# Attention with a gated MLP, one core: the steps of the plans in another order

## The chip, the cores and the metric

The kernel runs on one core of a Trainium2 chip. The metric is the device time of one execution in microseconds. The kernel before was timed in 11 runs; their median is 251.98 us, and they lie between 251.03 and 254.94 us. A separate execution was profiled: it gave the trace and the page of figures that this document reads.

The core has one engine for matrix products (PE, TensorE), with a part that loads its weights (PEld), two engines for elementwise work (DVE, VectorE, and ACT, ScalarE), a general one (POOL, GpSimd) and one that here only issues transfers (SP, SyncE). Each engine takes its instructions in a fixed order from its own queue. Engines wait for each other through semaphores.

## The reference

The inputs are q (8 batches, 16 heads, 384 positions, 64 wide), k and v (4 heads of the same size, each shared by four q heads), and the weights of a gated MLP: w_in 1024x1024, w_spatial 384x384 with a bias of 384, w_out 512x1024. Everything is float32. Cut to what matters:

```python
attn  = softmax(q @ k.T / 8)              # each k, v head serves four q heads
x     = (attn @ v), heads side by side    # [8, 384, 1024]
h     = relu(x @ w_in)                    # [8, 384, 1024]
u, v  = h[..., :512], h[..., 512:]
v_n   = (v - mean(v)) / sqrt(var(v) + 1e-6)      # over the 512
v_s   = w_spatial @ v_n + b_spatial       # mixes the 384 positions
out   = (u * v_s) @ w_out                 # [8, 384, 1024]
```

## The kernel before

**Plans.** The order of the work is written out by hand, as three strings of steps. `FIRST` holds batches 0 to 2 with the loading of the weights; `STEADY` is one repeating batch, run with the base batch 3, 4, 5 and 6; `LAST` is batch 7 and what is left of batch 6. `run` (lines 728 to 736) takes the steps of a string one after the other and calls a function for each. In a step such as `oc,-2,3,v` the first number is the batch relative to the base, and a letter at the end is the engine: v for DVE, s for ACT, p for POOL. All of it stands under a manual schedule, so each engine's queue holds its instructions exactly in the order of the plan. No scheduler moves anything. A step that stands earlier in the string stands earlier in its own engine's queue, and only there.

**What the steps do.** For each batch:
- `lq`, `lk`, `lv` load q (two halves of 8 heads), k and v in float32; they are issued on SP's queue. Each has one staging buffer, so a load waits until the casts of the batch before have read that buffer. `cq`, `ck`, `cv` cast to float16. `dk`, `dq` transpose k and q by DMA from SP's queue. The first two batches transpose on PE instead (`Tq`, `Tk`, with `tq`, `tk` to copy the result out of PSUM).
- `S` computes scores (two matmuls of 512 columns, line 367), `E` takes their exponentials on ACT (line 380). There are 18 of each per batch. They go through two score buffers in PSUM, so a score waits for the exponential two before it.
- `X` (lines 384 to 395) multiplies the exponentials with v for a tile of 128 positions. Parts 0 and 1 are the two halves of v's columns; part 2 multiplies with ones and so makes the sums of the softmax. All of them use strips of 32 columns of the array, so that four heads run side by side (line 394). `rl` and `re` make the reciprocal of the sums on ACT as exp(-ln) (lines 405 and 411), `rv` makes one on DVE, and `xm` multiplies a part with it on DVE (line 423).
- V is the half of h that becomes v; `ru` its relu (DVE line 448 or ACT line 450), `bs` its statistics (458, 459), `rs` the reciprocal root, `nm` the normalisation (469). `sa` adds the bias to the spatial product on DVE (495), `gt` is relu of u times v_s on DVE (521), `oc` copies a piece of the output out of PSUM (325 on ACT, 327 on DVE), `st` stores a pair of pieces from SP (563), and `lo` is the last piece.
- `lwi`, `lws`, `lwo` load the weights; `cws`, `cwo` cast them. w_out has two staging buffers for its four parts.

**Paired matmuls.** In a `G` step (lines 677 to 688) two streams of matmuls that use 64 rows each run at the same time in the upper and the lower half of the array. A `G` has two phases with two parts each. `w12`, `w24` and `w10` pair V of one tile (line 599) with two pieces of output of an earlier batch (line 639): `w12` is tile 2 of the batch before with pieces 2 and 3 of the batch before that, and so on. `gs` pairs spatial products (625), `gu` U products (612), `go` output products. The second phase swaps the halves of the array and must not begin before the first has ended. A mark (`mk`) sees to that:

```python
693: done = nc.vector.memset(mark_v[:, 0:1], 0.0)
695: done = nc.gpsimd.memset(mark_p[:, 0:1], 0.0)
```

The mark waits for the last matmul of the first phase, and the first matmul of the second phase waits for the mark. It stands in the queue of DVE or POOL like any other instruction: what is ahead of it delays it, and what is behind it waits for it.

**PSUM banks.** The results of `X`, V, U, spatial and output products share four banks. `bank` (lines 168 to 172) hands out the bank that was freed first, in the order in which the steps that read the results stand in the plan (`read`, lines 174 to 177). So which bank a product gets, and what it waits for, is settled by the order in the plan. Three buffers hold pairs of output pieces on their way to the store.

Of the kernel before, what the change touches and what calls it, by code (L numbers as in the profile page):

```python
# [774 lines left out]
```

## Time and profile before

| | us |
|---|---|
| median of 11 runs | 251.98 |
| lowest, highest | 251.03, 254.94 |
| the profiled execution, whole | 251.01 |
| its span in the trace | 249.2 |
| X,0,0,2 of batches 3, 4, 5, 6 starts at | 86.75, 115.20, 143.73, 172.33 |
| X,0,0,2 of the last batch starts at | 200.93 |
| last matmul ends | 244.98 |
| last store has landed | 248.07 |

The span runs from the first instruction to the last in the trace. The profiled execution took 1.81 us more than its span, which is what lies before and behind. A line of the profile's groups gives the line of the kernel, the engine, the operation, its output and inputs with their sizes, how often it ran, how long it was busy in all and on average, and how long the engine had been idle before it and for whom. A line of the timeline gives the start, the length and the same names, and, in brackets, the idle time just before. "Busy" of PE counts overlapping matmuls once. A row of the table by stretch gives the stretch, its length, the busy time and number of instructions of PE, PEld, DVE, ACT and POOL, then the granted clock of TensorE, the share of the 16 DMA engines' time and GB/s. "DMA" and "PEclk" in the page are tenths over 40 equal slices.

### The profile page before, as it was taken

The numbers are of one execution on the slowest core, as the hardware profiler recorded it, in microseconds if no ns is written. First come the engines' busy times: TensorE is split into PE (matmuls) and PEld (weight loads), VectorE is DVE, ScalarE is ACT, GpSimd is POOL, SyncE is SP. The second block draws the span as 40 slices with busy tenths as digits, with TensorE's granted clock in tenths as the row PEclk, the third lists the DMA queues.
The fourth block names the chain that finished last, engine by engine and source line by source line (L and its number), as shares of the span: only waits on it lengthen the run. The fifth ranks groups of instructions, "written<-read, shape, count | busy, mean of one in ns | idle before, by whom it ended". The sixth has DMA issues, their size and how long they took to land.

```text
span 249.2 us, 5953 instructions
## 1 busy us (share of the span) xinstructions
PE 238.4 (96%) x2505; PEld 122.2 (49%) x2505; DVE 148.4 (60%) x291; ACT 183.4 (74%) x231; POOL 48.2 (19%) x94
## 2 busy tenths in 40 slices
...
PEclk9999999999999999999999999999999999999999
DMA  7999999998799384771939366690932022200606
GB/s 184 272 253 321 188 255 292 235 312 143 88 323 325 93 206 122 239 227 73 208 116 308 93 163 166 178 284 13 200 120 87 3 84 87 85 3 0 252 0 252
DMA packets 57610, 42.71 MB, mean 171 GB/s; under 512 B 26864, under 2 KB 53872, under 8 KB 57584
## 3 DMA queue, kind: packets, MB, share of 16 engines
...
q14 instruction: 7, 0.06, 0.1%
...
## 4 chain that ended last, share of the span: by engine, by line
PE 91%; ACT 3%; DVE 2%; DMA 1%; issue 1%; ACTq 0%
PE X L394 20%; PE po L639 14%; PE sc L367 14%; PE pu L612 13%; PE pv L599 11%; PE pv L437 5%; PE psp L625 4%; PE po L544 4%; PE pu L509 4%; ACT aT L380 3%; DMA q<-in_q_dram 1%; DVE v_s L495 1%; PE pq L348 1%; PE psp L483 1%; PE sc_u L509 1%
## 5 line engine op out<-in xcount | busy, mean ns | idle before, releaser
L380 ACT ACTIVATE aT<-sc 128x1024 f16<-128x1024 f32 x144 | 140.2, 1025 | 28.0 <-PE sc L367 27.8
L639 PE MATMUL po<-w_out,gT 64*128 64x512 f16 x288 | 68.2, 376 | 0.0
L599 PE MATMUL pv<-w_in,xt 64*128 64x512 f16 x272 | 64.9, 376 | 0.0
L367 PE MATMUL sc<-qT,kT 64*128 64x512 f16 x288 | 54.8, 390 | 1.1 <-ACT aT L380 0.6
L327 DVE COPY osb<-po 128x512 f32<-128x512 f32 x39 | 26.9, 688 | 20.1 <-PE po L639 17.5
L394 PE MATMUL X<-aT,v 128*32 128x512 f16 x576 | 36.1, 380 | 0.0
L423 DVE TENSOR_TENSOR xt<-X,rec 128x512 f16<-128x512 f32 x48 | 31.1, 685 | 7.5 <-ACT rec L411 4.3
L612 PE MATMUL pu<-xt,w_in 64*128 64x384 f16 x384 | 35.4, 322 | 0.0
L639 PEld LDWEIGHTS <-gT 64*128 64x128 f16 x288 | 25.3, 94 | 14.6 <-DVE mark_v L693 3.0
L599 PEld LDWEIGHTS <-xt 64*128 64x128 f16 x272 | 24.7, 94 | 12.7 <-issue 4.2
L521 DVE SCALAR_TENSOR_TENSOR gT<-pu,v_s 128x384 f16<-128x384 f32 x31 | 16.1, 554 | 24.9 <-PE pu L612 21.1
L327 POOL CAST q<-q 128x768 f16<-128x768 f32 (+2 forms) x32 | 23.5, 761 | 32.1 <-DMA q<-in_q_dram 32.0
L367 PEld LDWEIGHTS <-kT 64*128 64x128 f16 x288 | 16.9, 94 | 24.2 <-issue 13.9
L612 PEld LDWEIGHTS <-w_in 64*128 64x128 f16 x384 | 18.8, 94 | 13.5
L495 DVE TENSOR_TENSOR v_s<-psp,bias_b 128x384 f32<-128x384 f32 x32 | 20.1, 689 | 6.1 <-PE psp L483 3.4
L394 PEld LDWEIGHTS <-v 128*32 128x32 f16 x576 | 15.9, 96 | 15.2 <-issue 2.6
L695 POOL MEMSET mark_p<- 1x1 f32 x18 | 1.6, 89 | 104.5 <-PE psp L625 64.5
L405 ACT ACTIVATE rec<-X 128x512 f32<-128x512 f32 x23 | 13.8, 599 | 9.2 <-PE X L394 8.5
L394 PE MATMUL X<-aT,ones 128*32 128x512 f16 x288 | 20.1, 382 | 0.5 <-DVE v_s L495 0.2
L458 DVE BATCH_NORM_STATS2 stats<-v_r 128x6 f32<-128x512 f32 x24 | 16.5, 689 | 5.5 <-ACT v_r L450 2.9
L625 PE MATMUL psp<-wsT,v_n 64*128 64x384 f16 x144 | 15.3, 323 | 0.1
L411 ACT ACTIVATE rec<-rec 128x512 f32<-128x512 f32 x23 | 14.5, 630 | 0.6
...
## 6 DMA issues: line engine op xcount, KB each, us to landing
...
```

Of the source, the lines that this page charges most:

```text
L327: engine.tensor_copy(dst, src)
L367: nc.tensor.matmul(sc[:, half, 0 : 512 // js], kT[b][lo:hi, gp, t, :], qT[b, gp][lo:hi, qt, j0::js], start=True, stop=True,)
L380: nc.scalar.activation(aT[b, qt][:, gp, t].rearrange("p h (j q) -> p h j q", j=G)[:, :, j0::js], held["sc", b, u, j0][:, :, 0 : 512 // js] ...
L394: nc.tensor.matmul(dst[32 * g : 32 * (g + 1), :], v16[:, g, t, 32 * part : 32 * (part + 1)] if part < 2 else ones32, a[:, g // 2, t, g % 2 ...
L423: nc.vector.tensor_tensor(xt[:, jj, :, qt * P : (qt + 1) * P], held["X", b, qt, jj].rearrange("p (j q) -> p j q", j=G), held["rec", b, qt] ...
L458: nc.vector.bn_stats(s6, held["v_r", b, st])
L495: nc.vector.tensor_tensor(held["v_s", b][:, m, :].rearrange("p (t s) -> p t s", t=NST), held["psp", b, m][:, 0:S].rearrange("p (t s) -> p ...
L521: nc.vector.scalar_tensor_tensor(held["gT", b][:, mu, :], held["pu", b, mu][:, 0:S], 0.0, held["v_s", b][:, mu, :], op0=ALU.max, op1=ALU.mult,
L599: yield lambda kc=kc: nc.tensor.matmul(held["pv", b, st], xT[b][rows, kc, st * P : (st + 1) * P], w_in16[rows, kc, DH:DFF], start=(first a ...
L612: yield lambda kc=kc: nc.tensor.matmul(held["pu", b, mu][:, 0:S], w_in16[rows, kc, mu * P : (mu + 1) * P], xT[b][rows, kc, :], start=(firs ...
L625: yield lambda st=st: nc.tensor.matmul(held["psp", b, m][:, 0:S], held["v_n", b, st][rows, m * P : (m + 1) * P], wsT16[rows, st, :], start ...
L639: yield lambda m=m: nc.tensor.matmul(held["po", b, i], held["gT", b][rows, m, tt * P : (tt + 1) * P], w_out16[rows, m, half * 512 : (half ...
```

## The change

Only the three strings differ. The set of steps is the same in each string, apart from the engine of some of them; what differs is their order.

In `STEADY`: `X,0,0,0` still follows the sums, but `X,0,0,1` is moved behind the first w phases, into the next tile; the parts of the next tile run as sums, the rest of the tile before, then its own; the scores `S` are spread in another way. The q casts are four as before, but one is on DVE instead of POOL and stands ahead of the w12 mark; one `ck` is on ACT instead of POOL; `ru,-1,2` and `oc,-2,3` are on ACT instead of DVE; the mark of `gs,2` is on DVE instead of POOL. `cv,1` is moved from the head of the batch to behind the mark of `gu,2` on POOL. The loads `lq,2,0`, `lv,2`, `lk,2` and `lq,2,1` are moved from the middle of the batch to its end, with v ahead of k, and the stores `st,-2` behind them.

In `LAST`: the products V of tiles 1 and 2 stand ahead of U of the batch before. U, spatial and output products of batches 6 and 7 stand in another order, and the stores are collected near the end; `st,0,1` comes after `lo`.

In `FIRST`: the first k and q loads change places, and so do the halves of the first casts; `lv,1` is ahead of q of batch 1; k of batch 2 is behind its q; w_out's loads come later, and so do their eight casts, six of them on POOL and two on DVE instead of six on POOL and two on ACT; the order of scores, exponentials and X parts differs throughout.

```diff
--- before
+++ after
 FIRST = """
-lq,0,0,0,1,0,1,s lk,0,0,2 cq,0,0,0,1,0,0,1,v lq,0,1,0,1 lk,0,2,4 ck,0,0,0,3,p cq,0,0,0,1,1,0,1,s
-Tq,0,0,0,0,1 Tk,0,0,0,3 tq,0,0,0,0,1,s lq,0,0,1,3 lq,0,1,1,3 tk,0,0,0,3,v S,0 ck,0,1,0,3,v
-cq,0,1,0,1,1,0,1,v cq,0,1,0,1,0,0,1,p lv,0 lk,1 S,0 lwi,0,1,0 lwi,0,1,2 Tk,0,1,0,3 lq,1,0 lq,1,1
-lws,0 cq,0,0,1,3,1,0,1,p lbi,0 lk,2 lv,1 Tq,0,1,0,0,1 lq,2,0 lwi,0,1,3 lwi,0,1,1 cq,0,1,1,3,0,0,1,p
-cq,0,1,1,3,1,0,1,p cv,0,p tk,0,1,0,3,v S,0 tq,0,1,0,0,1,v lq,2,1 lwo,0,1 cq,0,0,1,3,0,0,1,v E,0 E,0
...
-S,0 Tq,0,1,1,0,1 S,0 Tq,0,1,2,0,1 E,0 S,0 tq,0,1,2,0,1,v tq,0,1,1,0,1,v X,0,0,2 lwo,0,0
...
-cq,2,0,0,3,0,0,1,p cq,2,1,0,3,1,0,1,p cwo,0,1,1,p cwo,0,1,0,p cq,2,1,0,3,0,0,1,p xm,0,1,0 S,0
-tk,1,0,0,3,v cq,1,0,0,1,1,0,1,v cwo,0,0,0,p cwo,0,0,1,p S,0 E,0 Tk,1,1,0,3 V,0,1,0,4 Tq,1,0,0,0,1
...
-tq,1,1,1,0,1,s X,1,0,0 S,0 dk,2 bs,0,2 tw,0,0,2 dq,2,0 bs,0,0 S,0 X,1,0,1 Tq,1,1,2,0,1 rl,1,0 re,1,0
-lwo,0,3 lwo,0,2 xm,1,0,0 E,0 rs,0 xm,1,0,1 S,0 E,0 V,1,0,0,4 E,0 nm,0,0 nm,0,2 tq,1,1,2,0,1,v
-V,1,0,4,8 S,0 S,0 nm,0,1 G,0,gs,2,0,0,1 E,0 dq,2,1 ru,1,0,v E,0 G,0,gs,0,0,0,1 mk,0,gs,2,v
-mk,0,gs,0,v G,0,gs,2,1,0,1 S,0 G,0,gs,0,1,0,1 S,0 sa,0,2 sa,0,3 sa,0,0 sa,0,1 lk,3 lv,2 E,0 X,1,1,2
...
-G,0,gu,0,1,0 S,0 E,0 E,0 S,0 G,0,gu,0,1,1 G,0,gu,2,1,1 gt,0,1 gt,0,2 gt,0,3 E,0 E,0 S,0 cwo,0,3,0,p
-cwo,0,2,0,p X,1,2,2 X,1,2,1 V,1,1,0,4 V,1,1,4,8 S,0 E,0 rl,1,2 cwo,0,3,1,s gt,0,0 cwo,0,2,1,s re,1,2
-E,0 G,0,go,0,0,0 G,0,go,0,0,1 S,0 E,0 E,0 ru,1,1,v mk,0,go,0,v G,0,go,0,1,0 S,0 ck,3,0,0,3,p
...
-oc,0,2,v xm,2,0,0 G,1,w12,2,1,1 S,0 dk,3 dq,3,0 dq,3,1 lk,4 X,2,1,2 oc,0,3,v ru,1,2,v bs,1,2 X,2,1,1
...
-S,0 oc,1,0,v xm,2,2,0 X,2,2,1 st,0,1 st,0,0 E,0 lv,3 lq,4,0 st,0,2 ru,2,1,v oc,1,1,v lq,4,1 lv,4
...
+lk,0,0,2 lq,0,0,0,1,0,1,s cq,0,0,0,1,1,0,1,s lq,0,1,0,1 cq,0,0,0,1,0,0,1,v lk,0,2,4 ck,0,0,0,3,p
+Tq,0,0,0,0,1 Tk,0,0,0,3 tq,0,0,0,0,1,s lq,0,0,1,3 lq,0,1,1,3 tk,0,0,0,3,v lk,1 lv,0 ck,0,1,0,3,p S,0
+S,0 lv,1 Tk,0,1,0,3 cq,0,1,0,1,0,0,1,p cq,0,1,0,1,1,0,1,p lq,1,0 lws,0 lq,1,1 Tq,0,1,0,0,1 lbi,0
+lq,2,0 lq,2,1 lk,2 lwi,0,1,0 lwi,0,1,1 tk,0,1,0,3,v cq,0,0,1,3,1,0,1,p lwi,0,1,3 lwi,0,1,2
+tq,0,1,0,0,1,v cq,0,0,1,3,0,0,1,v E,0 S,0 S,0 ck,1,0,0,3,p ck,1,1,0,3,p cv,0,p Tq,0,0,2,0,1 E,0 E,0
...
+Tq,1,1,2,0,1 re,1,0 xm,1,0,0 S,0 E,0 xm,1,0,1 rs,0 E,0 nm,0,0 lwo,0,1 dq,2,0 nm,0,1 tq,1,1,2,0,1,v
+nm,0,2 lwo,0,0 dk,2 dq,2,1 lwo,0,2 lwo,0,3 V,1,0,0,4 lv,2 V,1,0,4,8 E,0 S,0 G,0,gs,2,0,0,1 S,0
...
+E,0 sa,0,3 sa,0,1 X,1,1,2 sa,0,0 E,0 rl,1,1 X,1,1,1 X,1,1,0 S,0 lq,3,1 lk,3 lq,3,0 re,1,1 E,0
...
+cwo,0,0,0,v G,0,gu,2,1,0 cwo,0,1,0,p cwo,0,0,1,p mk,0,gu,0,p cwo,0,1,1,p S,0 G,0,gu,0,1,0 S,0
+G,0,gu,0,1,1 E,0 gt,0,1 S,0 cwo,0,2,0,p E,0 G,0,gu,2,1,1 gt,0,2 gt,0,3 bs,1,0 gt,0,0 cwo,0,3,0,v E,0
+cwo,0,2,1,p S,0 X,1,2,2 X,1,2,1 E,0 cwo,0,3,1,p S,0 S,0 V,1,1,0,4 E,0 V,1,1,4,8 E,0 rl,1,2 S,0
+G,0,go,0,0,0 G,0,go,0,0,1 S,0 E,0 E,0 re,1,2 xm,1,2,1 mk,0,go,0,v E,0 G,0,go,0,1,0 E,0 S,0
...
+rl,2,1 bs,1,2 xm,2,0,1 re,2,1 S,0 xm,2,1,1 G,2,w24,0,0,0 G,2,w24,0,0,1 rs,1 S,0 E,0 S,0 E,0 E,0 lv,3
+xm,2,1,0 mk,2,w24,0,v dk,3 dq,3,0 dq,3,1 nm,1,2 nm,1,0 nm,1,1 G,2,w24,0,1,0 oc,0,4,v G,2,w24,0,1,1
...
+G,2,w10,1,1,1 S,0 X,2,2,1 E,0 oc,1,1,s lk,4 st,0,0 lq,4,0 st,0,2 lq,4,1 ru,2,1,v xm,2,2,1 oc,1,0,v
+st,0,1 E,0 bs,2,1 st,1,0 lv,4
 """
...
 STEADY = """
-X,0,0,2 rl,0,0 re,0,0 X,0,0,0 X,0,0,1 S,0 E,0 xm,0,0,0 xm,0,0,1 ck,1,0,0,3,p ck,1,1,0,3,p
-cq,1,0,0,3,0,0,1,p cq,1,0,0,3,1,0,1,p cq,1,1,0,3,0,0,1,p cq,1,1,0,3,1,0,1,p cv,1,p dk,1 dq,1,0
-dq,1,1 G,-1,w12,2,0,0 G,-1,w12,2,0,1 mk,-1,w12,2,v S,0 E,0 S,0 E,0 G,-1,w12,2,1,0 oc,-2,2,v
-G,-1,w12,2,1,1 ru,-1,2,v oc,-2,3,v st,-2,1 bs,-1,2 X,0,1,2 rl,0,1 re,0,1 X,0,1,0 X,0,1,1 rs,-1 S,0
-E,0 xm,0,1,0 xm,0,1,1 nm,-1,0 nm,-1,1 G,0,w24,0,0,0 G,0,w24,0,0,1 mk,0,w24,0,v nm,-1,2 S,0 E,0 S,0
-E,0 G,0,w24,0,1,0 oc,-2,4,v G,0,w24,0,1,1 ru,0,0,s oc,-2,5,v st,-2,2 bs,0,0 lk,2 lq,2,0 lq,2,1 lv,2
-S,0 E,0 G,-1,gs,0,0,0,1 mk,-1,gs,0,p S,0 E,0 G,-1,gs,2,0,0,1 mk,-1,gs,2,p G,-1,gs,0,1,0,1 sa,-1,0
-sa,-1,1 S,0 E,0 G,-1,gs,2,1,0,1 sa,-1,2 sa,-1,3 X,0,2,2 rl,0,2 re,0,2 X,0,2,0 X,0,2,1 S,0 E,0
-xm,0,2,0 xm,0,2,1 G,-1,gu,0,0,0 G,-1,gu,0,0,1 mk,-1,gu,0,p S,0 E,0 G,-1,gu,2,0,0 G,-1,gu,2,0,1
-mk,-1,gu,2,p S,0 E,0 G,-1,gu,0,1,0 G,-1,gu,0,1,1 gt,-1,0 gt,-1,1 S,0 E,0 G,-1,gu,2,1,0 G,-1,gu,2,1,1
-gt,-1,2 gt,-1,3 S,0 E,0 S,0 E,0 G,0,w10,1,0,0 G,0,w10,1,0,1 mk,0,w10,1,v S,0 E,0 S,0 E,0
-G,0,w10,1,1,0 oc,-1,0,v G,0,w10,1,1,1 ru,0,1,v oc,-1,1,v st,-1,0 bs,0,1 S,0 E,0
+X,0,0,2 cq,1,0,0,3,1,0,1,p cq,1,1,0,3,0,0,1,p cq,1,1,0,3,1,0,1,v X,0,0,0 rl,0,0 S,0 G,-1,w12,2,0,0
+G,-1,w12,2,0,1 cq,1,0,0,3,0,0,1,p ck,1,1,0,3,p dq,1,1 re,0,0 E,0 ck,1,0,0,3,s S,0 mk,-1,w12,2,v dk,1
+dq,1,0 S,0 G,-1,w12,2,1,0 G,-1,w12,2,1,1 E,0 xm,0,0,0 oc,-2,2,v X,0,1,2 E,0 ru,-1,2,s rl,0,1
+oc,-2,3,s re,0,1 X,0,0,1 X,0,1,0 bs,-1,2 xm,0,0,1 X,0,1,1 S,0 xm,0,1,0 G,0,w24,0,0,0 G,0,w24,0,0,1
+rs,-1 nm,-1,1 xm,0,1,1 mk,0,w24,0,v nm,-1,0 nm,-1,2 S,0 E,0 S,0 G,0,w24,0,1,0 oc,-2,4,v
+G,0,w24,0,1,1 E,0 E,0 S,0 G,-1,gs,0,0,0,1 S,0 ru,0,0,s mk,-1,gs,0,p oc,-2,5,v E,0 G,-1,gs,2,0,0,1
+bs,0,0 mk,-1,gs,2,v G,-1,gs,0,1,0,1 E,0 sa,-1,1 G,-1,gs,2,1,0,1 S,0 sa,-1,2 sa,-1,3 sa,-1,0 X,0,2,2
+rl,0,2 X,0,2,0 X,0,2,1 S,0 G,-1,gu,0,0,0 G,-1,gu,0,0,1 S,0 re,0,2 E,0 E,0 xm,0,2,0 xm,0,2,1 E,0
+G,-1,gu,2,0,0 G,-1,gu,2,0,1 S,0 mk,-1,gu,0,p E,0 G,-1,gu,0,1,0 G,-1,gu,0,1,1 S,0 E,0 mk,-1,gu,2,p
+cv,1,p G,-1,gu,2,1,0 G,-1,gu,2,1,1 S,0 S,0 gt,-1,0 gt,-1,1 gt,-1,3 gt,-1,2 G,0,w10,1,0,0
+G,0,w10,1,0,1 E,0 S,0 E,0 mk,0,w10,1,v S,0 G,0,w10,1,1,0 G,0,w10,1,1,1 oc,-1,0,v oc,-1,1,v ru,0,1,v
+lq,2,0 lv,2 lk,2 S,0 lq,2,1 st,-2,2 st,-2,1 E,0 E,0 E,0 bs,0,1 st,-1,0
 """
 
 LAST = """
-X,0,0,2 rl,0,0 re,0,0 X,0,0,0 X,0,0,1 S,0 E,0 xm,0,0,0 xm,0,0,1 G,-1,w12,2,0,0 G,-1,w12,2,0,1
-mk,-1,w12,2,v S,0 E,0 S,0 E,0 G,-1,w12,2,1,0 oc,-2,2,v G,-1,w12,2,1,1 ru,-1,2,v oc,-2,3,v st,-2,1
-bs,-1,2 X,0,1,2 rl,0,1 re,0,1 X,0,1,0 X,0,1,1 rs,-1 S,0 E,0 xm,0,1,0 xm,0,1,1 nm,-1,0 nm,-1,1
-G,0,w24,0,0,0 G,0,w24,0,0,1 mk,0,w24,0,v nm,-1,2 S,0 E,0 S,0 E,0 G,0,w24,0,1,0 oc,-2,4,v
-G,0,w24,0,1,1 ru,0,0,s oc,-2,5,v st,-2,2 bs,0,0 S,0 E,0 V,0,1,0,4 V,0,1,4,8 ru,0,1,s bs,0,1 SP,-1,0
-sa,-1,0 SP,-1,1 sa,-1,1 SP,-1,2 sa,-1,2 SP,-1,3 sa,-1,3 X,0,2,2 rl,0,2 re,0,2 X,0,2,0 X,0,2,1
-xm,0,2,0 xm,0,2,1 U,-1,0 gt,-1,0 U,-1,1 gt,-1,1 U,-1,2 gt,-1,2 U,-1,3 gt,-1,3 V,0,2,0,4 V,0,2,4,8
-ru,0,2,s bs,0,2 rs,0 nm,0,0 nm,0,1 nm,0,2 O,-1,0 oc,-1,0,s O,-1,1 oc,-1,1,s st,-1,0 O,-1,2 oc,-1,2,s
-O,-1,3 oc,-1,3,s st,-1,1 O,-1,4 oc,-1,4,s O,-1,5 oc,-1,5,s st,-1,2 U,0,0,1 SP,0,0 sa,0,0 gt,0,0
-SP,0,1 sa,0,1 SP,0,2 sa,0,2 SP,0,3 sa,0,3 U,0,1 gt,0,1 U,0,2 gt,0,2 U,0,3 gt,0,3 O,0,0,0,3 O,0,1,0,3
-O,0,0,3,4 oc,0,0,v O,0,1,3,4 oc,0,1,s st,0,0 O,0,2 oc,0,2,v O,0,3 oc,0,3,s st,0,1 O,0,4 oc,0,4,v
-st,0,2,0,512 lo,0,5
+S,0 X,0,0,2 E,0 G,-1,w12,2,0,0 G,-1,w12,2,0,1 S,0 mk,-1,w12,2,v S,0 E,0 rl,0,0 re,0,0 G,-1,w12,2,1,0
+G,-1,w12,2,1,1 S,0 X,0,1,2 oc,-2,2,v X,0,0,1 oc,-2,3,v rl,0,1 re,0,1 E,0 ru,-1,2,v X,0,1,1 X,0,0,0
+xm,0,0,1 xm,0,1,1 X,0,1,0 xm,0,0,0 S,0 G,0,w24,0,0,0 G,0,w24,0,0,1 E,0 mk,0,w24,0,v E,0 S,0 S,0 E,0
+bs,-1,2 xm,0,1,0 G,0,w24,0,1,0 G,0,w24,0,1,1 E,0 oc,-2,4,v ru,0,0,s X,0,2,2 rl,0,2 re,0,2 rs,-1
+oc,-2,5,s X,0,2,0 X,0,2,1 xm,0,2,0 xm,0,2,1 nm,-1,0 V,0,1,0,4 V,0,1,4,8 V,0,2,0,4 nm,-1,1 nm,-1,2
+U,-1,1 V,0,2,4,8 ru,0,1,s SP,-1,0 SP,-1,1 bs,0,0 ru,0,2,v sa,-1,0 sa,-1,1 bs,0,2 gt,-1,1 bs,0,1
+U,-1,0 SP,-1,2 SP,-1,3 rs,0 nm,0,1 sa,-1,2 sa,-1,3 nm,0,0 nm,0,2 gt,-1,0 U,0,0,1 U,-1,2 gt,-1,2
+U,-1,3 SP,0,2 gt,-1,3 sa,0,2 SP,0,3 O,-1,4 U,0,2 SP,0,0 sa,0,3 sa,0,0 O,-1,2 O,-1,0 oc,-1,4,v gt,0,2
+O,-1,1 oc,-1,0,s oc,-1,1,s O,-1,5 O,-1,3 SP,0,1 oc,-1,5,v oc,-1,2,v sa,0,1 U,0,1 U,0,3 gt,0,0 gt,0,1
+gt,0,3 oc,-1,3,s st,-2,2 O,0,0,0,3 st,-2,1 st,-1,2 O,0,4 O,0,1,0,3 oc,0,4,s O,0,0,3,4 O,0,1,3,4
+st,-1,1 st,-1,0 oc,0,1,v oc,0,0,s O,0,2 O,0,3 oc,0,2,s oc,0,3,s st,0,2,0,512 st,0,0 lo,0,5 st,0,1
 """
```

## The prediction

> **What bounds the kernel now.** I read the page first, then the busy times by stretch, then TensorE's timeline of one repeating batch, and last the queues that feed it.
>
> ```profile
> span 249.2 us, 5953 instructions
> PE 238.4 (96%) x2505; PEld 122.2 (49%) x2505; DVE 148.4 (60%) x291; ACT 183.4 (74%) x231; POOL 48.2 (19%) x94
> ...
> PEclk9999999999999999999999999999999999999999
> DMA  7999999998799384771939366690932022200606
> ...
> PE 91%; ACT 3%; DVE 2%; DMA 1%; issue 1%; ACTq 0%
> ```
>
> TensorE holds 91% of the chain at full granted clock. The DMA row is at nines up to 60 us, and loose afterwards. The busy times by stretch:
>
> ```profile
> 115.20:143.80 28.60, 28.54 (x333) 15.69 (x336) 17.72 (x35) 22.26 (x27) 5.24 (x11) 1.00 0.66 174
> 143.80:172.40 28.60, 28.54 (x333) 15.69 (x336) 17.72 (x35) 22.26 (x27) 5.24 (x11) 1.00 0.62 173
> ```
>
> A repeating batch takes 28.60 us. Since matmuls overlap, "28.54 busy" hides waits, so I sum the issue spacings instead: a 512-column pair or round is 0.216, a 384-column pair 0.1625, a switch between X (32-column strips) and anything else about 0.1 (X from 143.73 to the score at 145.79: 2.06 for 9 rounds, 1.94). A batch is 9 X parts at 0.65, 18 scores at 0.216, six w phases at 1.73, four gs phases at 0.49, four gu phases at 1.30: 27.22, with six switches 27.8. So **0.8 us of each batch are waits**, and only these can be won. TensorE's timeline of the batch that starts at 143.73 shows where:
>
> ```profile
> 146.02 0.38 PE L639 MATMUL po<-w_out,gT 64*128 64x512 f16 x1
> 146.24 0.38 PE L639 MATMUL po<-w_out,gT 64*128 64x512 f16 x1
> ...
> 146.79 0.37 PE L639 MATMUL po<-w_out,gT 64*128 64x512 f16 x1
> ...
> 158.74 0.72 PE L625 MATMUL psp<-wsT,v_n 64*128 64x384 f16 x6
> 159.52 0.83 PE L394 MATMUL X<-aT,ones 128*32 128x512 f16 x12
> ```
>
> The third po of w12 should start at 146.45; it waits 0.34 for its bank, which xm,0,0,0 (DVE, 146.05, 0.69 long) reads out. From there to the next X (150.33) w12 takes 4.31 where its matmuls need 3.99: 0.32 lost. w24 (152.62 to 156.62) loses 0.1 to 0.2 in the same way, on xm,0,1,0. X,0,2,2 at 159.52 should follow the psp by 0.59; it waits 0.2 for the bank that sa,-1,0 frees. The rest is thinly spread.
>
> **The change part by part.** No instruction is added or removed: matmuls, casts, copies and bytes are the same, so all of it is in waits, in five places. Let t = 0 be X,0,0,2 of a batch.
>
> *Repeating batch, four of them.* The new order on TensorE: X,0,0,2 at 0; X,0,0,0 at 0.65; score; w12 from 1.61, second phase 3.77; four X from 5.6; score; w24 from 8.5 to 12.5; gs 12.8 to 15.2; X,0,2; gu; w10. By the banks of the new order, w12 takes those freed by oc,-1,1, by ru,0,1 and by rl,0,0. DVE copies at 0.6 each behind the end of w10: oc,-1,0 at -0.3, oc,-1,1 at 0.6, ru at 1.2; rl on ACT ends at 1.7 (ACT's last exponential ends 1.1 after X starts, as at 144.86, then 0.59). The third pair stands at 2.04: nothing waits. What stays is the mark (0.43 of scores cover about 0.53): 0.1. **Gain 0.2.** In w24 the third pair still needs xm,0,1,0. rl,0,1 starts 0.9 after X,0,1,2 (207.53 to 208.41 in the trace) at 6.6; oc,-2,3, now on ACT ahead of re, adds 0.6; re ends at 8.45, xm at 9.15; the third pair stands at 9.04, because three X parts now run behind the sums instead of two. Same loss. At gs, X,0,2,2 waits for sa,-1,1 instead of sa,-1,0, with one gs phase and a score as cover: 0.15 instead of 0.2. Moving one ck (0.5), ru (0.6) and oc (0.6) to ACT is covered: ACT is idle for 1.25 before 148.50 and 0.93 before 154.96. Sum -0.25 a batch, **-1.0 for four**.
>
> *The loads of the batch after next.* This is the part that can bite. The steps lq,2,0 lv,2 lk,2 lq,2,1 move to the end; lv waits for cv,1, which now stands behind mk,-1,gu,2 on POOL instead of at the batch's start, and lk, lq,2,1 and the two stores st,-2 queue behind it on SP. Before:
>
> ```profile
> 128.93 0.33 SPq L563 DMA_DIRECT2D out_dram<-osb  x1
> 129.32 0.43 SPq L203 DMA_DIRECT2D k<-in_k_dram  x1
> 129.79 1.87 SPq L217 DMA_DIRECT2D q<-in_q_dram  x2
> 131.76 1.64 SPq L210 DMA_DIRECT2D v<-in_v_dram  x1
> ```
>
> These issue 14 us ahead of the batch at 143.73, and POOL's q casts begin at 137.93. After the change: that mark is at -7.4 (136.31 in the trace), cv takes 0.83, lv issues at -6.4, lk at -6.0, lq,2,1 at -5.5. When does that q land? [...] q after q landed 2.4 apart (POOL waits that end 137.93 and 140.22), so v 1.2, k 1.2, q 2.4 and 2.6 until the first arrives: **+1.0**. I take the rows. One cast of it, cq,1,1,0,3,1, is now DVE's, ahead of the w12 mark, and the other is POOL's at the same moment. DVE is free at 2.0 (bs,0,1 is 0.87). The skill ("SBUF — State Buffer", Who interferes with whom) says that such a DVE copy and a GpSimd instruction block each other for the whole instruction; the rows of 128x512 casts on DVE are 0.46 alone, 0.63 and 0.94 beside POOL's. For 768 columns: 0.7 alone, 1.4 beside; by the rule, with POOL's cast (0.84) first at 1.0, it is over before DVE starts. I take 1.0, to 3.0; the mark is due at 3.5. **Cost 0**, with 0.5 to spare: the load may land up to 2.6. Transposes (dq, dk) then issue at 3 to 8 instead of 1.6 to 6.4, land about 4 to 5 later, and their scores stand at 13: covered. Osb's three buffers: st,-2,1 lands near 4, its buffer is written at 4.8: covered by 0.8.
>
> *First part.* It has two switches less (-0.2). Against it: two k16 halves and q casts swapped between DVE and POOL at the start delay the third score by 0.2 while ACT is the bound (exponentials without a break from 6.96); a q cast (0.42) stands before the seventeenth exponential; the go mark stands behind xm,1,2,1: 0.4. For it: two w_out casts (1.14) leave ACT. DMA order: k of batch 2 moves behind its q's, v of batch 1 ahead, w_out's last halves issue near 47.5 instead of 43.0 because cwo,0,1,1 stands behind a mark on POOL; they landed 5.9 after issue, which with casts is just the 54 at which go needs them (0 to 0.5). Net of waits +0.2. **Sum 0** (-0.7 to +1.0).
>
> *Last batch.* X to the end of the matmuls is 44.05 (200.93 to 244.98); its matmuls need 42.9, after 43.0. Waits 1.1 before. After: w12 and w24 0.35. Then V precedes U, and DVE has ru, two sa, bs, gt, bs, the 0.61 until rstd is there (229.03 to 229.64), nm and sa in a row: U,-1,3 waits 0.25 for sa,-1,2; SP,0,3 0.25 for gt,-1,0; O,-1,0 0.1. **-0.1** (±0.6).
>
> *Tail.* Stores are moved on SP: st,0,1 (512 KB) is now issued behind the last piece. Before, SP's last issue is at 245.33 and ACT's at 245.47, landing 2.6 later. After, st,0,1 goes out 0.8 after the last matmul instead of 0.5, and is four times as long: **+0.6** (0.3 to 1.0).
>
> Sum: -1.0 + 0 - 0.1 + 0.6 = -0.5. The profiled execution took 251.01 in all, so 250.5. It is the fastest of what was run: the median of the 11 runs is 251.98. One spot explains that: the transposed q of batch 2 is issued at 39.92, lands 7.9 later and is first needed at 48.43, 0.6 us to spare with the DMA row at nines. In the new order fewer bytes stand ahead of it (neither k of batch 2 nor v of batch 1), an estimate of 5 us earlier. So I expect the median near the profile's time: **250.6**.
>
> **The rivals.**
> *A: as summed*, 250.6, from 249.2 (half of the batches' waits gone too) to 251.2 (bounds of first part and tail). For it: the bank waits named.
> *B: given back.* The last batch's DVE row, go's late w_out and the tail cost 0.5 each more, or the gap between profile and median stays: 251.6. For it: the first part had few waits left, so a new order finds more easily than it removes. Against: ACT is less loaded there.
> *C: the late loads decide, and it is slower.* If q lands as late after its issue as the slowest row of the batches (9.4), it is there at 3.9, the DVE cast ends at 4.9, and the mark, and behind it w12's second phase, start 1.1 late, in the three batches whose q is loaded that way: +3.3, 253.9; it decides from 2.6 on. For it: two of three batches landed in over 8. Against: there 1.7 MB went ahead, here 0.8.
>
> **How the numbers follow.** A 0.52, B 0.20, C 0.28. A measurement of this kernel tells from no change only 0.5% (1.26 us), so faster is below 250.7, slower above 253.2: A is faster in 0.46 and same in 0.06, B the same, C slower. Faster 0.46, same 0.26, slower 0.28. Range 249.0 to 254.2: A's lower end, and C with its cast blocked beside POOL's.
>
> **What would show it.** Right: batches of 28.3 to 28.4; no jump at w12's third po; DVE's q cast starting below 2.6 after X,0,0,2; the store of 512 KB last on SP. Wrong: DVE idle on "DMA q" at a batch's start; go waiting for w_out near 54; U,-1,3 waiting more than 0.5; a first part that ends later than now (X,0,0,2 of batch 3 at 86.75).

## The result, and the profile after

The changed kernel takes 249.74 us in the median of 13 runs (249.22 to 251.10). The kernel before takes 251.52 us in the median of the 48 runs taken beside it and earlier (250.82 to 254.94). The ratio is 0.9923, with a 95% interval of 0.9903 to 0.9943: 0.8% faster, 1.8 us. The forecast was 250.6, with a range of 249.0 to 254.2.

The profiled execution of the changed kernel took 249.97, its span is 248.2; before it was 251.01 and 249.2. These lines of the page answer to those shown of before:

```profile
span 248.2 us, 5946 instructions
PE 237.4 (96%) x2505; PEld 112.7 (45%) x2505; DVE 147.1 (59%) x293; ACT 187.8 (76%) x242; POOL 42.0 (17%) x81
...
PEclk9999999999999999999999999999999999999999
DMA  7999999997799059229980779419924020030075
...
PE 89%; DMA 5%; DVE 1%; ACT 1%; issue 1%; SPq 0%; POOL 0%; DVEq 0%; POOLq 0%
```

TensorE sets the end as before, at the full granted clock. One figure is new: 5% of the chain, some 12 us, is now a transfer, against 1% before. The page's list by line gives all of it to q<-in_q_dram. Of this, 3.6 us lie at the very start, as before; 8.66 us are new and lie in one piece, from the issue of a q load at 138.02 to its landing at 146.68, which is 3.12 us into the third repeating batch. The busy times by stretch, from one X,0,0,2 to the next, show what that does:

```profile
87.44:115.50 28.06, 28.02 (x333) 13.68 (x326) 17.47 (x35) 23.25 (x30) 1.82 (x5) 1.00 0.57 152
115.50:143.56 28.06, 28.02 (x330) 13.60 (x328) 17.47 (x35) 23.42 (x30) 3.87 (x8) 1.00 0.66 176
143.56:172.08 28.52, 28.19 (x330) 13.59 (x328) 17.42 (x35) 23.42 (x30) 3.87 (x8) 1.00 0.68 172
172.08:200.05 27.97, 27.93 (x331) 13.79 (x330) 17.35 (x35) 23.42 (x30) 3.10 (x7) 1.00 0.45 135
```

The first number after the stretch is its length. A batch took 28.60 before, and the first 28.45: the rows of TensorE have X,0,0,2 of batches 3 and 4 at 86.68 and 115.13, and the 86.75 and 115.20 given ahead of the prediction are 0.07 too late. Three of four now take 28.06 or less, and the third takes 28.52. In the third, DVE and then TensorE wait for that q:

```profile
146.77 0.95 DVE L326 CAST q<-q 128x768 f16<-128x768 f32 x1 [1.10 <-DMA q<-in_q_dram]
147.67 0.06 DVE L692 MEMSET mark_v<- 1x1 f32 x1
147.81 0.39 PE L638 MATMUL po<-w_out,gT 64*128 64x512 f16 x1 [0.29 <-DVE mark_v L692]
```

The last row of the table by stretch ends at the score with which `LAST` now begins.

The two spans, cut at the same places, account for the whole difference:

| part | before | after | difference | forecast |
|---|---|---|---|---|
| first part, to X,0,0,2 of batch 3 | 86.68 | 87.44 | +0.76 | 0 (-0.7 to +1.0) |
| four repeating batches | 114.25 | 112.61 | -1.64 | -1.0 |
| last batch, to the last matmul's end | 44.05 | 43.52 | -0.53 | -0.1 |
| last matmul's end to the last landing | 3.09 | 3.53 | +0.44 | +0.6 |
| sum | 248.07 | 247.10 | -0.97 | -0.5 |

### The profile page after: what moved, and what is told of

The parts are those of the page before. It is cut to its first block, busy times and chain, and to the rows that moved or that the text cites. A ratio compares the mean times of both kernels' runs of the same rounds, so it can differ in the third digit from the quotient of the medians.

```text
span 248.2 us, 5946 instructions
## 1 busy us (share of the span) xinstructions
PE 237.4 (96%) x2505; PEld 112.7 (45%) x2505; DVE 147.1 (59%) x293; ACT 187.8 (76%) x242; POOL 42.0 (17%) x81
## 4 chain that ended last, share of the span: by engine, by line
PE 89%; DMA 5%; DVE 1%; ACT 1%; issue 1%; SPq 0%; POOL 0%; DVEq 0%; POOLq 0%
PE X L393 20%; PE sc L366 14%; PE po L638 12%; PE pu L611 12%; PE pv L598 11%; PE pv L436 5%; DMA q<-in_q_dram 5%; PE psp L624 4%; PE po L543 4%; PE pu L508 4%; PE pq L347 2%; PE psp L482 2%; DVE v_s L494 1%; ACT aT L379 1%; PE sc_u L508 1%
## 5 line engine op out<-in xcount | busy, mean ns | idle before, releaser
L638 PE MATMUL po<-w_out,gT 64*128 64x512 f16 x288 | 66.4, 376 | 0.3 <-DVE mark_v L692 0.3
L598 PE MATMUL pv<-w_in,xt 64*128 64x512 f16 x272 | 64.2, 376 | 0.0
L366 PE MATMUL sc<-qT,kT 64*128 64x512 f16 x288 | 52.1, 393 | 0.7 <-DVE kT L326 0.5
L422 DVE TENSOR_TENSOR xt<-X,rec 128x512 f16<-128x512 f32 x48 | 31.8, 683 | 12.0 <-ACT rec L410 6.4
L326 DVE COPY osb<-po 128x512 f32<-128x512 f32 x34 | 23.3, 690 | 16.6 <-PE po L638 11.0
L598 PEld LDWEIGHTS <-xt 64*128 64x128 f16 x272 | 25.2, 94 | 14.7 <-issue 0.8
L326 POOL CAST q<-q 128x768 f16<-128x768 f32 (+2 forms) x27 | 19.7, 749 | 46.3 <-DMA q<-in_q_dram 39.8
L366 PEld LDWEIGHTS <-kT 64*128 64x128 f16 x288 | 15.0, 94 | 25.4 <-issue 14.3
L324 ACT ACTIVATE osb<-po 128x512 f32<-128x512 f32 x13 | 7.7, 595 | 14.7 <-PE po L543 14.7
```

What stands on the lines that cost most here:

```text
L326: engine.tensor_copy(dst, src)
L366: nc.tensor.matmul(sc[:, half, 0 : 512 // js], kT[b][lo:hi, gp, t, :], qT[b, gp][lo:hi, qt, j0::js], start=True, stop=True,)
L422: nc.vector.tensor_tensor(xt[:, jj, :, qt * P : (qt + 1) * P], held["X", b, qt, jj].rearrange("p (j q) -> p j q", j=G), held["rec", b, qt] ...
L598: yield lambda kc=kc: nc.tensor.matmul(held["pv", b, st], xT[b][rows, kc, st * P : (st + 1) * P], w_in16[rows, kc, DH:DFF], start=(first a ...
L638: yield lambda m=m: nc.tensor.matmul(held["po", b, i], held["gT", b][rows, m, tt * P : (tt + 1) * P], w_out16[rows, m, half * 512 : (half ...
```

## The experiments

In the text below "lowest" is the lowest of a kernel's runs. The runs of the kernel before spread unevenly: of the 99 taken beside these experiments, 22 lie more than 2 us above the lowest of those taken with them. Where a median moves less than a lowest, this spread is why.

**The three strings, one at a time.** `only_first`, `only_steady` and `only_last` are the kernel before with one string taken from the changed kernel:

```diff
-FIRST, STEADY, LAST of the kernel before
+FIRST of the changed kernel, STEADY and LAST of the kernel before      (only_first)
+STEADY of the changed kernel, FIRST and LAST of the kernel before      (only_steady)
+LAST of the changed kernel, FIRST and STEADY of the kernel before      (only_last)
```

> FIRST of the change alone; STEADY and LAST as before. By the two traces (X,0,0,2 of batch 3 at 86.68 before, 87.44 after) FIRST costs 0.76 us in an undisturbed execution: X,0,0,2 of batch 3 at 87.4, span near 250.0. Theory 'transposed q of batch 2': the kernel before loses a median of 0.5 and up to 4 us beyond its fastest runs where that q is late, and the new order of the loads takes this away; then the runs lie close together (spread under 2 us instead of 4) and the median is 251.5 to 252.0. Rival 'the first part was the gain': median below 251.0. Rival 'spread comes from elsewhere': median 252.3 with runs up to 255.

Measured: 251.87 in the median (251.54 to 252.99), ratio 0.9991 [0.9957, 1.0026]. The lowest is 0.72 above the lowest of before, and no run is more than 1.5 above the lowest. Both halves of the expectation came out: `FIRST` costs 0.7, and with it the runs lie close together.

> STEADY of the change alone. By the traces four batches take 112.6 instead of 114.25 (28.06 a batch against 28.6, one of them 28.52 on a late q): -1.65 us, so a median near 249.9 if the runs of before are its reference at 251.5. X,0,0,2 of batch 3 stays at 86.7, that of the last batch is at about 199.4. The spread stays wide (to 253 or more) if it comes from FIRST. Rival 'the order of the batches gives little, and the measured difference is the first part's': 251.2 or more.

Measured: 250.75 (249.69 to 253.69), ratio 0.9946 [0.9905, 0.9987]. Faster, but by 0.7 in the median and 1.1 in the lowest, not by 1.65. Its trace says where the rest is: the first of the four batches takes 28.72 instead of 28.06, and the last 28.48 on a late q (landed 3.1 behind its X,0,0,2). The first one is taken up below (`best`).

> LAST of the change alone. By the traces its matmuls end 0.53 earlier from where they begin, and the last store lands 3.53 instead of 3.09 behind the last matmul: -0.1 us net, 251.4. My forecast had -0.1 +0.6 = +0.5, 252.0. The wide spread of before stays.

Measured: 251.07 (250.70 to 254.48), ratio 0.9940 [0.9902, 0.9979]. The lowest is 0.12 below that of before, as the traces have it; the median is 0.4 below. The +0.5 of my forecast is refuted. This trace also holds the one look at what the forecast said of the first part: a run of 252.0 with `FIRST` of before. TensorE's timeline:

```profile
47.89 1.46 PE L611 MATMUL pu<-xt,w_in 64*128 64x384 f16 x16
49.68 0.61 PE L366 MATMUL sc<-qT,kT 64*128 64x512 f16 x4 [0.33 <-DMA qT<-q]
```

Here the transposed q of batch 2 landed at 49.55, and the score that needs it waited: the sixteen U products before it end 1.30 after their start where nothing waits, and here the score starts 1.79 after. That is 0.49 us lost, of the 1.0 by which this run lies over the profiled run of before.

**What the gain in the batches is.** Two kernels ask whether it comes from the bank that `X,0,0,1` holds, or from the lighter queues of DVE and POOL. `x_back` takes the changed kernel and undoes this move, together with the multiplication and the reciprocal that go with it:

```diff
-X,0,0,2 cq,1,0,0,3,1,0,1,p cq,1,1,0,3,0,0,1,p cq,1,1,0,3,1,0,1,v X,0,0,0 rl,0,0 S,0 G,-1,w12,2,0,0
-G,-1,w12,2,0,1 cq,1,0,0,3,0,0,1,p ck,1,1,0,3,p dq,1,1 re,0,0 E,0 ck,1,0,0,3,s S,0 mk,-1,w12,2,v dk,1
-dq,1,0 S,0 G,-1,w12,2,1,0 G,-1,w12,2,1,1 E,0 xm,0,0,0 oc,-2,2,v X,0,1,2 E,0 ru,-1,2,s rl,0,1
-oc,-2,3,s re,0,1 X,0,0,1 X,0,1,0 bs,-1,2 xm,0,0,1 X,0,1,1 S,0 xm,0,1,0 G,0,w24,0,0,0 G,0,w24,0,0,1
+X,0,0,2 cq,1,0,0,3,1,0,1,p cq,1,1,0,3,0,0,1,p X,0,0,0 X,0,0,1 rl,0,0 re,0,0 xm,0,0,0 cq,1,1,0,3,1,0,1,v S,0 G,-1,w12,2,0,0
+G,-1,w12,2,0,1 cq,1,0,0,3,0,0,1,p ck,1,1,0,3,p dq,1,1 E,0 ck,1,0,0,3,s S,0 mk,-1,w12,2,v dk,1
+dq,1,0 S,0 G,-1,w12,2,1,0 G,-1,w12,2,1,1 E,0 xm,0,0,1 oc,-2,2,v X,0,1,2 E,0 ru,-1,2,s rl,0,1
+oc,-2,3,s re,0,1 X,0,1,0 bs,-1,2 X,0,1,1 S,0 xm,0,1,0 G,0,w24,0,0,0 G,0,w24,0,0,1
```

> The changed kernel with X,0,0,1 put back ahead of w12 in STEADY, its multiplication xm,0,0,0 with it ahead of the w12 mark, and the reciprocal ahead of the exponential, as before; everything else of the change stays. Theory 'bank wait': the third pair of w12 again waits for the bank that xm,0,0,0 reads, so w12's first phase takes 1.87 instead of 1.73, the scores at the mark 0.53 instead of 0.43, the second phase 1.9 instead of 1.82: +0.3 a batch, +1.2 in all, 250.9. Rival 'the gain of the batches comes from the other engines' lighter queues (ru, oc, ck on ACT, mark on DVE)': batches stay at 28.06, 249.7.

Measured: 252.52 (251.76 to 253.71), ratio to the kernel before 1.0041 [1.0010, 1.0073]: 2.8 us over the changed kernel, more than the 1.2 expected, and slower than before. TensorE's timeline of one batch of `x_back`, at w12 and then at w24:

```profile
119.69 0.38 PE L638 MATMUL po<-w_out,gT 64*128 64x512 f16 x1
119.90 0.38 PE L598 MATMUL pv<-w_in,xt 64*128 64x512 f16 x1
120.24 0.37 PE L638 MATMUL po<-w_out,gT 64*128 64x512 f16 x1
...
126.29 0.38 PE L638 MATMUL po<-w_out,gT 64*128 64x512 f16 x1
126.50 0.38 PE L598 MATMUL pv<-w_in,xt 64*128 64x512 f16 x1
127.04 0.37 PE L638 MATMUL po<-w_out,gT 64*128 64x512 f16 x1 [0.17 <-DVE xt L422]
```

The same place in the changed kernel, where the two streams stay even:

```profile
117.35 0.38 PE L638 MATMUL po<-w_out,gT 64*128 64x512 f16 x1
117.57 0.38 PE L598 MATMUL pv<-w_in,xt 64*128 64x512 f16 x1
117.57 0.38 PE L638 MATMUL po<-w_out,gT 64*128 64x512 f16 x1
```

The jump at the third pair is back: po starts at 120.24, where its partner pv started at 119.90, and in w24 at 127.04 instead of 126.50, where the trace names the multiplication on DVE. Measured from step to step, the jump costs three times. In w12 the first phase takes 1.87 instead of 1.73, the two scores at the mark 0.53 instead of 0.43, and the second phase 1.92 instead of 1.82: once one stream of the pair lags, the phase ends late, the mark comes late, and the second phase begins with its streams apart. That is 0.34, as expected. In w24 the first phase takes 2.07 instead of 1.73 and the scores 0.53 instead of 0.43, another 0.44, which I had not expected. The kernel before lost only 0.10 there; in `x_back` the copy `oc,-2,3` stands on ACT ahead of the reciprocal, which so ends 2.49 behind X,0,1,2 instead of 2.15, and the multiplication comes later by as much. Together this is 0.78 of the 0.80 by which the batch is longer (28.86 against 28.06). So without this one move, the rest of the change makes a batch longer than before (28.60).

`x_alone` does the reverse, that one move alone in the kernel before:

```diff
-X,0,0,2 rl,0,0 re,0,0 X,0,0,0 X,0,0,1 S,0 E,0 xm,0,0,0 xm,0,0,1 ck,1,0,0,3,p ck,1,1,0,3,p
+X,0,0,2 rl,0,0 re,0,0 X,0,0,0 S,0 E,0 xm,0,0,0 ck,1,0,0,3,p ck,1,1,0,3,p
...
-G,-1,w12,2,1,1 ru,-1,2,v oc,-2,3,v st,-2,1 bs,-1,2 X,0,1,2 rl,0,1 re,0,1 X,0,1,0 X,0,1,1 rs,-1 S,0
-E,0 xm,0,1,0 xm,0,1,1 nm,-1,0 nm,-1,1 G,0,w24,0,0,0 G,0,w24,0,0,1 mk,0,w24,0,v nm,-1,2 S,0 E,0 S,0
+G,-1,w12,2,1,1 ru,-1,2,v oc,-2,3,v st,-2,1 bs,-1,2 X,0,1,2 rl,0,1 re,0,1 X,0,0,1 X,0,1,0 X,0,1,1 rs,-1 S,0
+E,0 xm,0,0,1 xm,0,1,0 xm,0,1,1 nm,-1,0 nm,-1,1 G,0,w24,0,0,0 G,0,w24,0,0,1 mk,0,w24,0,v nm,-1,2 S,0 E,0 S,0
```

> The kernel before with one part of STEADY's change alone: X,0,0,1 and its xm,0,0,1 move behind w12, into the next tile. FIRST, LAST, engines, loads and all else as before. Theory 'bank wait' (putting X,0,0,1 back cost the changed kernel 0.75 a batch): w12's phases take 1.73 and 1.82 and the scores at its mark 0.43 as in the changed kernel, -0.33 a batch; w24 the same or up to 0.1 less; batches of 28.1 to 28.3, so 1.3 to 1.9 us faster than before: 249.6 to 250.2. Rival 'it takes the relu, copy and mark moved to other engines too': batches of 28.5 or 28.6, 251.4.

Measured: 250.82 (249.98 to 253.47), ratio 0.9966 [0.9926, 1.0007]. The median alone doesn't settle it, the trace does. Busy times of one batch of `x_alone`, in the columns used above:

```profile
115.99:144.13 28.14, 28.07 (x331) 15.34 (x330) 17.71 (x35) 22.23 (x27) 5.25 (x11) 1.00 0.67 177
```

28.14 with all engines as before (POOL still has 11 instructions, ACT 27), against 28.60 before and 28.06 in the changed kernel. Its w12 and w24 phases and the scores between them take what they take in the changed kernel (1.73, 0.43, 1.82, and 1.73, 0.43, 1.73). So **0.46 of the 0.54 us of a batch is this one move**; the casts, relus, copies and marks on other engines are worth at most the other 0.08, which lies at `gs`. DVE's queue did not hold up the w12 mark in the kernel before either: DVE stood idle for 0.96 ahead of it, waiting for the matmuls. The first batch of `x_alone` takes 28.79, which is why its median gains little; that is the wait at the seam, where `FIRST` passes over to `STEADY`, that `best` shows.

**The late q.** `cv_early` moves one step of the changed `STEADY`, `cv,1`, back to the head of the batch, so that v, k and q of the batch after next are issued much earlier:

```diff
-G,-1,w12,2,0,1 cq,1,0,0,3,0,0,1,p ck,1,1,0,3,p dq,1,1 re,0,0 E,0 ck,1,0,0,3,s S,0 mk,-1,w12,2,v dk,1
+G,-1,w12,2,0,1 cq,1,0,0,3,0,0,1,p ck,1,1,0,3,p cv,1,p dq,1,1 re,0,0 E,0 ck,1,0,0,3,s S,0 mk,-1,w12,2,v dk,1
...
-cv,1,p G,-1,gu,2,1,0 G,-1,gu,2,1,1 S,0 S,0 gt,-1,0 gt,-1,1 gt,-1,3 gt,-1,2 G,0,w10,1,0,0
+G,-1,gu,2,1,0 G,-1,gu,2,1,1 S,0 S,0 gt,-1,0 gt,-1,1 gt,-1,3 gt,-1,2 G,0,w10,1,0,0
```

> The changed kernel with one step of STEADY moved: cv,1 on POOL stands at the batch's head, behind ck,1,1, and no longer behind the mark of gu,2. So lv, lk and lq,2,1 of the batch after next are issued some 17 us earlier. Theory 'late q': in the trace of the changed kernel q landed 2.7, 3.1 and 1.3 us behind X,0,0,2 of three batches, and the second of them lost 0.46 by DVE's cast ahead of the w12 mark; here no q is late, every batch takes 28.06: 0.3 to 0.6 us faster than the changed kernel, 249.2 to 249.5. Rival 'the loads now collide with the transposes and the q casts of the same batch': a batch of 28.3 or more somewhere, not faster than the changed kernel.

Measured: 249.58 (249.38 to 250.47, 6 runs), ratio 0.9878 [0.9827, 0.9928]. X,0,0,2 follows X,0,0,2 by 28.05, 28.06 and 28.05: no batch loses anything. The medians differ by 0.2 in favour of `cv_early`, less than these runs can tell apart. `q_late` goes the other way: the q load stands behind two stores on SP.

```diff
-lq,2,0 lv,2 lk,2 S,0 lq,2,1 st,-2,2 st,-2,1 E,0 E,0 E,0 bs,0,1 st,-1,0
+lq,2,0 lv,2 lk,2 S,0 st,-2,2 st,-2,1 lq,2,1 E,0 E,0 E,0 bs,0,1 st,-1,0
```

> The changed kernel with one step of STEADY moved: lq,2,1 stands behind the stores st,-2,2 and st,-2,1 on SP, so 1 MB of stores goes ahead of that q. Theory 'late q by way of DVE's cast ahead of the w12 mark, from 2.6 us on': the q lands about 2.4 us later than in the changed kernel (2.7, 3.1, 1.3 behind X,0,0,2), near 5.1, 5.5 and 3.7, and the three batches lose 2.4, 2.8 and 1.0: +5.5 us over the changed kernel, 255. Rival 'a late q is covered by other work': under 1 us slower, 250.5.

Measured: 252.94 (252.20 to 253.27), ratio to before 1.0036 [1.0007, 1.0066]; 3.2 us over the changed kernel, slower than before. The theory's place is right and its size was too large, because the q landed 0.9, 1.1 and 2.2 us later and not 2.4. It was also issued 1.03 later, so in two of the three batches having 1 MB of stores ahead of it instead of behind it cost at most 0.1 beyond the later issue. The timelines of DVE and TensorE in the middle batch of `q_late` (X,0,0,2 at 144.65):

```profile
146.57 0.18 DVE L458 BATCH_NORM_AGGREGATE mv<-stats 128x2 f32<-128x6 f32 x1
148.99 0.95 DVE L326 CAST q<-q 128x768 f16<-128x768 f32 x1 [2.23 <-DMA q<-in_q_dram]
149.87 0.69 DVE L422 TENSOR_TENSOR xt<-X,rec 128x512 f16<-128x512 f32 x1
149.88 0.06 DVE L692 MEMSET mark_v<- 1x1 f32 x1
150.02 0.39 PE L638 MATMUL po<-w_out,gT 64*128 64x512 f16 x1 [1.41 <-DVE mark_v L692]
```

DVE stands idle for the q, casts it, sets the mark, and only then may TensorE go on. The two kernels give six points, four of them with a loss. "Landed" is the landing of q behind X,0,0,2, "lost" what the scores at the w12 mark take beyond 0.43:

| kernel, batch | landed | lost | landed - lost |
|---|---|---|---|
| changed, 4 | 2.67 | 0.00 | |
| changed, 5 | 3.12 | 0.45 | 2.67 |
| changed, 6 | 1.31 | 0.00 | |
| q_late, 4 | 3.55 | 0.91 | 2.64 |
| q_late, 5 | 4.25 | 1.57 | 2.68 |
| q_late, 6 | 3.50 | 0.82 | 2.68 |

So the late load decides from about 2.67 us on, and every microsecond beyond costs one: 3.3 us in the three batches of `q_late`, 0.45 in the changed kernel.

**The tail of the runs.** The forecast put the gap between the profiled run and the median of before down to the transposed q of batch 2. `q2_first` takes k of batch 2 out of its way in the kernel before, and `q2_w_in` also issues two loads of w_in earlier:

```diff
-lws,0 cq,0,0,1,3,1,0,1,p lbi,0 lk,2 lv,1 Tq,0,1,0,0,1 lq,2,0 lwi,0,1,3 lwi,0,1,1 cq,0,1,1,3,0,0,1,p
-cq,0,1,1,3,1,0,1,p cv,0,p tk,0,1,0,3,v S,0 tq,0,1,0,0,1,v lq,2,1 lwo,0,1 cq,0,0,1,3,0,0,1,v E,0 E,0
+lws,0 cq,0,0,1,3,1,0,1,p lbi,0 lv,1 Tq,0,1,0,0,1 lq,2,0 lwi,0,1,3 lwi,0,1,1 cq,0,1,1,3,0,0,1,p
+cq,0,1,1,3,1,0,1,p cv,0,p tk,0,1,0,3,v S,0 tq,0,1,0,0,1,v lq,2,1 lk,2 lwo,0,1 cq,0,0,1,3,0,0,1,v E,0 E,0
...
-ck,1,1,0,3,v ck,2,1,0,3,p ck,2,0,0,3,p cq,1,1,1,3,0,0,1,p lwi,0,0,0 cv,1,p cq,2,0,0,3,1,0,1,p
-cq,2,0,0,3,0,0,1,p cq,2,1,0,3,1,0,1,p cwo,0,1,1,p cwo,0,1,0,p cq,2,1,0,3,0,0,1,p xm,0,1,0 S,0
+ck,1,1,0,3,v cq,1,1,1,3,0,0,1,p lwi,0,0,0 cv,1,p cq,2,0,0,3,1,0,1,p
+cq,2,0,0,3,0,0,1,p ck,2,1,0,3,p ck,2,0,0,3,p cq,2,1,0,3,1,0,1,p cwo,0,1,1,p cwo,0,1,0,p cq,2,1,0,3,0,0,1,p xm,0,1,0 S,0
...
-tq,1,1,1,0,1,s X,1,0,0 S,0 dk,2 bs,0,2 tw,0,0,2 dq,2,0 bs,0,0 S,0 X,1,0,1 Tq,1,1,2,0,1 rl,1,0 re,1,0
+tq,1,1,1,0,1,s X,1,0,0 S,0 bs,0,2 tw,0,0,2 dq,2,0 dk,2 bs,0,0 S,0 X,1,0,1 Tq,1,1,2,0,1 rl,1,0 re,1,0
```

and in `q2_w_in` besides:

```diff
-cq,1,0,1,3,1,0,1,p cq,1,1,0,1,0,0,1,p lwi,0,0,1 lwi,0,0,3 cws,0,0 lwi,0,0,2 rv,0,0 S,0 X,0,0,1 E,0
+cq,1,0,1,3,1,0,1,p lwi,0,0,1 lwi,0,0,3 cq,1,1,0,1,0,0,1,p cws,0,0 lwi,0,0,2 rv,0,0 S,0 X,0,0,1 E,0
```

> The kernel before with one part of FIRST changed: k of batch 2 is loaded behind both halves of its q, cast behind the two q casts of gp 0, and transposed behind dq,2,0. STEADY and LAST as before. Theory 'the transposed q of batch 2 makes the slow tail of the kernel before': in the trace of only_last it landed at 49.55 and the U products stood 0.49 us for it, in the traces with the new FIRST it landed at 42.3 to 43.8, five us ahead of its need. Here 384 KB and one transpose (1.3 us of issue) are no longer ahead of it: it lands near 45, no run is over 252.5, lowest near 250.9, median 251.1. Rival 'the tail comes from w_in, w_spatial or the start of the loads': the tail to 254 stays, in about 3 of 10 runs.

Measured: 251.87 (251.15 to 253.54), ratio 1.0015 [0.9982, 1.0048]. The edit failed in what it was to do: the transposed q landed at 47.51, against 47.78 before. Four of 12 runs lie more than 2 us above the lowest. So this run tells nothing for or against the theory.

> The kernel q2_first with two loads of w_in (lwi,0,0,1 and lwi,0,0,3 on POOL) ahead of the q cast before them, so that they are issued at about 21 instead of 24 and less stands beside batch 2's q. STEADY and LAST as before. In q2_first the transposed q of batch 2 was issued at 39.60 and landed at 47.51, 0.3 earlier than before, and the tail stayed. Theory 'the tail is that landing': here it lands near 44 to 45 and no run is above 252.5, median 251.1 to 251.4. Rival 'the tail is something else in FIRST': it lands as early, and 3 or 4 of 12 runs still lie above 252.9.

Measured: 251.80 (250.99 to 253.69), ratio 1.0014 [0.9987, 1.0041]. In its profiled run the q landed at 44.29, as wanted, 4.5 us ahead of its need, and still 2 of 12 runs lie 2.3 and 2.7 above the lowest. The theory isn't upheld as the whole cause, though none of the slowest executions was itself traced. What stands is the count by kernel: with `FIRST` of before or a variant of it 16 of 84 runs of the experiments lie over 2 us above their kernel's lowest; with `FIRST` of the change, the changed kernel's own runs included, 3 of 63, all of one kernel (`cv_tail`), whose single lowest run is 0.74 below its next. So the tail goes with the order of `FIRST`, and which load in it makes it is open.

**Parts together.** `best` joins `STEADY` with the early `cv`, `LAST` with another order of the stores, and `FIRST` of `q2_first`:

```diff
-st,-1,1 st,-1,0 oc,0,1,v oc,0,0,s O,0,2 O,0,3 oc,0,2,v oc,0,3,s st,0,2,0,512 st,0,0 lo,0,5 st,0,1
+st,-1,1 st,-1,0 oc,0,1,v oc,0,0,s O,0,2 O,0,3 oc,0,2,v oc,0,3,s st,0,0 st,0,1 st,0,2,0,512 lo,0,5
```

> STEADY of the change with cv,1 at the batch's head, LAST of the change with the stores st,0,0 and st,0,1 ahead of the last two pieces, and FIRST of before with batch 2's q ahead of its k (as in q2_first). If the parts add up: from the lowest of before, 250.8, less 1.9 for four batches at 28.06, less 0.5 for LAST, tail as before: 248.4 lowest, 248.6 median. Rival 'what FIRST lost is found elsewhere': not under 249.5.

Measured: 250.08 (249.74 to 252.78), ratio 0.9943 [0.9908, 0.9978]. The rival held: what was left out at the start came back behind it. TensorE's timeline of its first repeating batch (X,0,0,2 at 86.90), at w12:

```profile
88.53 0.38 PE L598 MATMUL pv<-w_in,xt 64*128 64x512 f16 x1
89.20 0.37 PE L638 MATMUL po<-w_out,gT 64*128 64x512 f16 x1 [0.30 <-DVE xt L422]
```

It is the bank wait again, at the seam. The banks are handed out in the order of the plan, and with the end of `FIRST` of before a pair of w12 gets the bank that `xm,2,2,1` reads, which DVE begins only at 88.49, behind `bs,2,1`. The batch takes 28.71; `only_steady` and `x_alone` lose the same in the same place. So 0.66 of the gain of the changed kernel's batches rests on the end of its own `FIRST`. The stores didn't help either: the last piece's own store, now behind all others on SP, is issued 0.68 behind the last matmul's end (0.05 in the changed kernel), and lands 3.87 behind it.

`cv_tail` is `cv_early` with the stores in a third order, and `best2` is `cv_tail` with `FIRST` of `q2_w_in` and `xm,2,2,1` ahead of `bs,2,1`:

```diff
-st,-1,1 st,-1,0 oc,0,1,v oc,0,0,s O,0,2 O,0,3 oc,0,2,v oc,0,3,s st,0,2,0,512 st,0,0 lo,0,5 st,0,1
+st,-1,1 st,-1,0 oc,0,1,v oc,0,0,s O,0,2 O,0,3 oc,0,2,v oc,0,3,s st,0,2,0,512 st,0,0 st,0,1 lo,0,5
```

and in `best2` besides:

```diff
-cv,3,p bs,2,1 xm,2,2,1 E,0 st,1,0
+cv,3,p xm,2,2,1 bs,2,1 E,0 st,1,0
```

> The changed kernel with cv,1 at the batch's head (as in cv_early) and, in LAST, the store st,0,1 ahead of the last piece instead of behind it. In the changed kernel st,0,1 is issued 0.4 us behind the last piece's own store and lands last, 3.53 us behind the last matmul. Here it is issued at about -0.2, and the last landing is that of ACT's piece, 2.9 to 3.0 behind the last matmul: -0.6 against cv_early, 249.0. Rival 'the store of 512 KB collides with the last pieces': they land 0.5 later and nothing is won, 249.6.

Measured: 249.47 (248.44 to 250.83), ratio 0.9907 [0.9869, 0.9946]. The last landing is 3.23 behind the last matmul's end instead of 3.53. Half of what was expected: the last two pieces land 2.78 after their issue, where ACT's took 2.43 and SP's 1.74 with the big store behind them, so there is some collision.

> STEADY and LAST as in cv_tail; FIRST as in q2_w_in, with xm,2,2,1 ahead of bs,2,1. In the kernel best the first repeating batch lost 0.66 in w12, whose third pair waited for the bank that xm,2,2,1 reads; here that multiplication is 0.85 us earlier, and the batch takes 28.06. Against cv_tail the faster start of FIRST gives another 0.5 to 0.7: 248.3 to 248.6 in the median. Rival 'the bank wait at the seam is not that one, or FIRST of before keeps its tail': batch 3 at 28.5 or more, or runs above 251.

Measured: 249.15 (248.51 to 250.76), ratio 0.9916 [0.9889, 0.9943]. Its four batches take 28.05, 28.06, 28.06 and 27.95, so the seam is repaired and the reason for it shown. Its median is the lowest of all, by 0.6 under the changed kernel, but its interval covers that of the changed kernel (0.9903 to 0.9943), and so it isn't shown to be faster.

## Why the prediction was right or wrong

**What bounds the kernel: right.** Waits on TensorE's path moved the time, and at the end the last store. ACT is 4.4 us busier in the page and DVE 1.3 us less busy, and neither shows in a batch.

**Repeating batch, -0.25 each: right in mechanism, too small.** Undisturbed batches gained 0.54. The forecast named the wait of w12's third pair for `xm,0,0,0` and its new bank; `x_alone` and `x_back` show that this is the cause. Three terms were too small. In w12 I kept 0.1 for the mark, and it is 0: that 0.1 was a consequence of the lag between the streams, not of the mark, since two scores take 0.43 as soon as the streams are even. In w24 the step "Same loss" failed: the forecast put the end of `xm,0,1,0` at 9.15 behind X,0,0,2, and it ended at 8.82 (124.32), ahead of the third pair at 8.98, because the reciprocal ended at 8.1 and not at 8.45: I had added up whole lengths of about 0.6 on ACT, and its rows start 0.49 and 0.48 apart (122.00, 122.49, 122.97). The third pair in time is worth 0.10. At `gs` 0.09 was won instead of 0.05.

**The loads: the mechanism right, "Cost 0" wrong by 0.46.** The forecast let q land at +1.0 with room to 2.6. It landed at 2.67, 3.12 and 1.31; the limit is about 2.67. The failing term is the spacing on the queue: I took 2.4 us between k's landing and q's, from two q loads in a row, and it was 4.3, 5.0 and 3.2 (113.85 to 118.17, 141.64 to 146.68, 170.15 to 173.39). I had counted only what stands ahead of that q on the queue. The two stores behind it are issued 0.6 after it and are in flight with it; in `cv_early`, where they follow 2.3 or more after it, k and q land 2.3, 2.7 and 2.4 apart. That makes the stores the likely cause, but no run changes them alone. The rule of the Trainium skill that I weighed ("SBUF — State Buffer", Who interferes with whom) ties the blocking to a DVE copy in one of its two-port modes. It doesn't show in the time of this cast:

```profile
89.70 0.95 DVE L326 CAST q<-q 128x768 f16<-128x768 f32 x1
...
118.25 0.95 DVE L326 CAST q<-q 128x768 f16<-128x768 f32 x1 [0.64 <-DMA q<-in_q_dram]
```

These rows of DVE's timeline are of the changed kernel. At 89.70 POOL had been idle for 6 us; at 118.25 it was casting two q pieces itself, from 118.22 on for 1.60 us, 0.80 each. Both casts of DVE take 0.95; which mode they ran in, no run shows. My 0.7 alone and 1.4 beside POOL were both wrong, and the 1.0 that I took was right by luck. I had scaled them from casts of 128x512; the casts of 128x384 on DVE in the trace of before took 0.49 and 0.54 with POOL idle, and would have given about 1.0.

**Rival C: real, and nearer than its time said.** With 0.28 it stood for 253.9, slower than before. `q_late`, one step away from the changed kernel, shows it: 252.94, by just that chain of waits. In the changed kernel it took 0.46 of one batch in the profiled run.

**First part, 0: inside its bounds.** It costs 0.76 in the two traces. Over all profiled runs, from ACT's first exponential to X,0,0,2 of batch 3, the eight kernels with `FIRST` of before or a variant of it take 79.7 to 81.0 (median 79.7), the six with that of the change 80.1 to 81.2 (median 80.4): 0.7. The forecast had seen a delay of the third score, 0.2; the tenth exponential begins 8.4 behind the first before and 9.2 after, in the medians, so in the medians most of the 0.7 arises there, but not in each trace: `cv_tail` is at 8.5 there and still takes 80.1. The two switches saved and the casts moved off ACT didn't make up for it. The loads of w_out, feared to be late for go, were not.

**Last batch, -0.1: right in sign, too small (-0.53).** The busy row on DVE cost less than feared: U,-1,2 and U,-1,3 lost 0.07 together, where 0.25 was allowed for, and the spatial products behind them 0.17. w12 and w24 gained as in the repeating batches, 0.43: they keep 0.1 of waits where I had left 0.35.

**Tail, +0.6: right (+0.44).** `st,0,1` is issued at 244.04, 0.02 after ACT's last piece, and lands last, 3.06 later.

**Median near the profiled time: right as a number, not as a cause.** The median lies 0.2 below the profiled run now and lay 0.5 above it before. The transposed q of batch 2 lands at 42.32 instead of 47.78, so the 5 us of the estimate were good; but `q2_w_in` brought it forward too and kept a tail. Of the 1.78 us between the medians, 1.04 is the difference of the two profiled runs, and the rest this spread.

So the likeliest case came true, 0.86 below its time: 0.64 from the batches, 0.43 from the last batch and 0.16 from the tail, less 0.76 for the first part; 0.33 because the median lies 0.23 below its profiled run where I had allowed 0.1 above; and the rest from the time ahead of the span and behind the last landing. Part of that is luck: errors of both signs. Two of the signs that were to show it wrong did appear: DVE idle on the q at a batch's start (0.64 and 1.10), and a first part that ends later.
